# Ten channel chunks of a token-and-channel mixer as five pairs in one stage, with the first block's up-projection issued from the attention stage

## The chip, the cores and the metric

The program runs on one core of one Trainium2 chip. The metric is device time in microseconds (us). Three runs of the kernel before took 1213.01, 1213.05 and 1217.84 us; the median is 1213.05 us. All arithmetic is in 32-bit floating point. A matmul operand is split into a high and a low part, and a product of two operands is three matmuls (high by high, high by low, low by high).

## What is computed

Three blocks follow one another on 8 sequences of 576 tokens with 512 channels.

```python
# 1. memory attention: 8 sequences, 8 heads, 576 x 64, 32 memory slots
a = softmax(phi); k_m = a.T @ k; v_m = a.T @ v
x = softmax(q @ k_m.T * scale) @ v_m
# 2. mixer: tokens 576 -> 256 -> 576, channels 512 -> 1536 -> 512
u = x + (relu(x.T @ w_tok1) @ w_tok2).T
x = u + relu(u @ w_ch1) @ w_ch2
# 3. four attention heads, causal, gated: the two best of four for each token
out = sum over the chosen heads of gate * (softmax(causal(q k.T)) @ v @ wo)
```

The change concerns the channel part, `relu(u @ w_ch1) @ w_ch2`. Its 1536 hidden channels are 12 chunks of 128. An up-projection multiplies u with one chunk of `w_ch1`; a down-projection multiplies the result with the same chunk of `w_ch2` and adds it to a sum over chunks.

## The kernel before, in words

**Stage 1, attention and tokens.** The work is 16 units, one for each sequence and each half of its heads. A unit has a front (`front`, L340: phi's maximum, the exponential, k_m and v_m, q transposed), rows (`rows`, L476: scores, softmax, transposes back) and a mix (`mix`, L568: both token matmuls, then u). A unit uses every engine several times in turn: PE, DVE, ACT and POOL. The loads of phi, k, v and q go through SP (`loads`, L313); u is kept in an SBUF tile `u1` for each sequence and stored to `u_d` (`u_s`, L633).

Chunks 0 and 1 of the channel part are done here too (N1 = 2, L245). `block(j)` (L659) does one half sequence, 288 tokens: it splits u (`u_hi`, `u_lo`, L663 to L670), does two up-projections (`up`, L672; `up_hi`, `up_lo`) and four partial sums of the down-projection (`down`, L691), adds them to u (`down_c`, L696) and stores u plus the partial sum to `p_d` (`store`, L700). One block is 48 matmuls of 288 columns. There are 16 blocks. Those of the last sequence (`rest`, L734) are not planned in stage 1; they are issued at the start of stage 2 (L1068).

The weights arrive as 64-bit numbers. `convert` (L746) turns a piece into a high and a low part: one DMA into a staging tile `cst` (three of them), two ACT instructions, four DVE instructions, and a last subtraction on POOL or DVE. In stage 1 that happens to the token weights (5 pieces) and to chunks 0 to 6 of the channel weights (7 chunks, 14 pieces, `chan`, L814).

The order of stage 1 is written out ahead of time by a planner (`Plan`, L63). Each task carries an engine, an assumed duration, what it reads and writes, and a place in a ring of buffers (L304). The planner issues, on each engine, the ready task with the lowest rank: the latest start that its successors allow, or `due` where one is given. The order it finds is then kept on each engine.

**Stage 2, channels** (L898 to L1162). Nine blocks of 512 tokens are multiplied with chunks 2 to 9, as four pairs. `mm1` (L916) is the up-projection of one chunk, 12 matmuls of 512 columns; `mm2` (L1019) is the down-projection of one chunk, 12 matmuls of 512 columns into four PSUM banks. In blocks 2 to 7 (`WIDE`), `mm1w` (L980) does the two up-projections of a pair with seven products instead of eight quarter-products: 42 matmuls of 256 columns. For that, sums of weights are formed during block 1 (`sums_w`, L935) and sums of u before each wide block (`split_q`, `split_t`). A down-projection is issued one step after its up-projection. At the end of a block `load_p` (L1029) has brought u plus the partial sum from `p_d`, DVE adds the four banks, and the result goes to `x_d` (L1026, L1027). `midload` (L1062) converts the weights of chunks 7 to 9 during block 0 (`f64_split`, L223). Instructions outside the planned stage are put in order by the framework's own scheduler, which may move them ahead of their place in the text when their data and memory are free.

**Stage 3, the last two chunks and the heads** (from L1166). Chunks 10 and 11, then the third block. The change does not touch it.

Of the kernel before, what the change touches and what calls it, by code (L numbers as in the profile page):

```python
# [9 lines left out]
F32 = mybir.dt.float32  # L10
# [52 lines left out]
class Plan:  # L63
# [5 lines left out]
    def add(self, eng, ns, fn, reads=(), writes=(), take=None, n=1, kind="", due=None):  # L69
        t = dict(i=len(self.tasks), eng=eng, ns=ns, fn=fn, take=take, n=n, kind=kind, due=due, pre=set(), gives=[], holders=0)  # L70
# [19 lines left out]
    def order(self):  # L90
# [26 lines left out]
        for t in ts:  # L117
            if not left[t["i"]]:
                open_[t["eng"]].append(t["i"])
        wire, now = 0, 0  # L120
# [47 lines left out]
def fused_kernel(ctx: ExitStack, tc, q, k, v, phi, w_tok1, w_tok2, w_ch1, w_ch2,  # L168
# [19 lines left out]
    p_d = tc.dram_tile([DM, NT], F32, name="p_d")  # L188
# [56 lines left out]
    N1, NP, N3 = 2, 5, 2  # L245
    KM = KF - N3
    wch_ctx, b1_ctx, stg_ctx = ExitStack(), ExitStack(), ExitStack()
    wbm = wch_ctx.enter_context(tc.tile_pool(name="wbm", bufs=1, reuse_waits="tile"))
    wb = b1_ctx.enter_context(tc.tile_pool(name="wb", bufs=1, reuse_waits="tile", side="right"))
    wk1 = None  # L250
    ppb1 = b1_ctx.enter_context(tc.tile_pool(name="ppb1", bufs=1, space=PSUM, reuse_waits="tile", side="right"))
# [18 lines left out]
    u1, uh1, ul1, h1 = {}, {}, {}, {}  # L270

    def half(j):
        return slice(SH * (j % 2), SH * (j % 2) + SH)

    with ExitStack() as sa:
        wk1 = b1_ctx.enter_context(tc.tile_pool(name="wk1", bufs=1, reuse_waits="tile", side="right"))
        wa = sa.enter_context(tc.tile_pool(name="wa", bufs=1, reuse_waits="tile"))
        stg = stg_ctx.enter_context(tc.tile_pool(name="stg", bufs=2, reuse_waits="tile", side="right"))
        ld = sa.enter_context(tc.tile_pool(name="ld", bufs=1, reuse_waits="tile"))
        wk_ = sa.enter_context(tc.tile_pool(name="wk_", bufs=1, reuse_waits="tile"))  # L280
        pp = sa.enter_context(tc.tile_pool(name="pp", bufs=1, space=PSUM, reuse_waits="tile"))
# [17 lines left out]
        DVE.memset(kv_[ST:128, :, :, 4, :], 0.0)  # L299

        units = [(b, g) for b in range(B) for g in range(2)]
        NU, NR, NJ = len(units), 2, 2 * B
        NB = S // 32
        plan = Plan(pools=dict(t=2, g=4, b=2, cst=3, cy=2, cm=2),  # L304
# [8 lines left out]
        def loads(n):  # L313
            b, g = units[n]
            hs = slice(4 * g, 4 * g + 4)

            def l_phi():
                t, src = phb[n % NB2], phi[b, hs]
# [1332 lines left out]
```

## Time and profile before

| | before |
|---|---|
| median of three runs | 1213.05 us |
| the profiled execution: its own time | 1214.76 us |
| the profiled execution: its span | 1213.0 us |
| PE busy, share of the span | 1165.3 us, 96% |
| DVE busy | 816.3 us, 67% |
| ACT busy | 610.8 us, 50% |
| POOL busy | 449.5 us, 37% |
| mean share of the 16 DMA engines in use | 39.2% |

The profile is one execution. PE is the matmul engine, DVE the vector engine, ACT the scalar engine, POOL the general engine, SP the one that issues the DMAs here. Busy time is the union of an engine's instructions in a stretch. A granted clock of 1.00 means that PE ran at the upper of its two levels (2.4 GHz) in the whole stretch; 0.74 means that it ran at the lower one (1.2 GHz) in about half of it. The mean duration of a PE matmul in a table is longer than the distance from one to the next, since matmuls overlap; in the chain of waits the distance is seen. "PE o" are down-projections of stage 2, "PE h" its up-projections, "PE b" the matmuls of `block`.

### The profile page before, as it was taken

How to read it: one execution, taken by the hardware profiler on the slowest of the kernel's cores; microseconds unless marked ns; L12 is line 12 of the kernel's file. 1: busy time of each engine (PE TensorE's matmuls, PEld its weight loads, DVE VectorE, ACT ScalarE, POOL GpSimd, SP SyncE). 2: the span in 40 equal slices, each digit the busy share in tenths (PEclk: the TensorE clock that was granted, in tenths of full speed). 3: DMA queues.
4: the chain of work that ended last, by engine and by line, in shares of the span. 5: the costliest groups of instructions: out<-in, count | busy, mean ns of one | idle time of the engine just before them, and what ended most of it. 6: DMA issues, size and time to landing. Idle time of an engine off the chain costs nothing.

```text
span 1213.0 us, 23508 instructions
## 1 busy us (share of the span) xinstructions
PE 1165.3 (96%) x8586; PEld 1064.7 (88%) x8586; DVE 816.3 (67%) x1992; ACT 610.8 (50%) x1591; POOL 449.5 (37%) x603
## 2 busy tenths in 40 slices
PE   4899998999999999999999999999999999999998
PEld 3678887999888888889999889999999999999986
DVE  6999998665483756567566514777676767676664
ACT  3565565454442323223322213677676767677775
POOL 2774453442002012112111344545454627383331
PEclk9799999999999999999999999999999999999999
DMA  8896767532370221232123343322333333322522
GB/s 239 251 276 209 215 212 221 171 118 92 97 251 20 105 70 35 71 104 97 43 71 105 96 113 114 88 84 79 84 88 83 102 97 99 94 80 54 166 86 105
DMA packets 133780, 145.07 MB, mean 120 GB/s; under 512 B 35616, under 2 KB 101408, under 8 KB 133664
## 3 DMA queue, kind: packets, MB, share of 16 engines
q1 hardware_dynamic: 133664, 143.57, 39.2%
q8 instruction: 68, 1.11, 0.4%
q14 instruction: 48, 0.39, 0.1%
HBM read 91.10 MB, written 40.89 MB: 109 GB/s over the span
## 4 chain that ended last, share of the span: by engine, by line
PE 79%; DVE 11%; DMA 3%; issue 2%; ACT 2%; POOL 1%; SPq 0%; DVEq 0%; ACTq 0%; POOLq 0%
PE g L207 21%; PE o L207 16%; PE h L207 16%; PE y L1423 4%; PE b L207 3%; PE s L1314 3%; PE b L679 3%; PE t L1378 3%; PE s L1336 1%; DVE ul L670 1%; DVE cy L772 1%; PE g L623 1%; PE g L383 1%; PE g L624 1%; PE g L626 1%
## 5 line engine op out<-in xcount | busy, mean ns | idle before, releaser
L1359 POOL TENSOR_TENSOR a<-a,cf 128x128 f32<-128x128 f32 (+3 forms) x128 | 88.3, 723 | 68.9 <-DVE cf L1351 64.9
L207 PE MATMUL o<-hl,w2h 128*128 128x512 f32 x288 | 112.7, 391 | 0.3 <-DVE hl L931 0.3
L207 PE MATMUL o<-hh,w2l 128*128 128x512 f32 x288 | 112.3, 390 | 0.0
L207 PE MATMUL o<-hh,w2h 128*128 128x512 f32 x288 | 108.7, 392 | 0.2 <-DVE pb L1026 0.2
L930 ACT ACTIVATE hh<-m 128x256 fp32r<-128x256 f32 x96 | 38.9, 416 | 111.8 <-DVE m L1001 72.2
L1303 DVE CUSTOM_DVE_ANT_0 ssb<-s,cmask 128x128 f32<-128x128 f32 (+2 forms) x144 | 68.5, 483 | 27.3 <-PE s L1314 20.5
L1316 ACT ACTIVATE a<-ssb,nb 128x128 f32<-128x128 f32 (+3 forms) x128 | 71.3, 558 | 18.4 <-DVE nb L1303 15.1
L207 PE MATMUL h<-uh,w1h 128*128 128x512 f32 (+2 forms) x200 | 66.5, 334 | 4.7 <-ACT uh L211 4.7
L931 DVE SCALAR_TENSOR_TENSOR hl<-m,hh 128x256 fp32r<-128x256 f32 x96 | 58.2, 615 | 17.6 <-ACT hh L930 15.4
L978 POOL TENSOR_TENSOR tl<-ub,th 128x512 fp32r<-128x512 f32 x12 | 18.1, 1526 | 136.3 <-ACT th L977 136.3
L207 PE MATMUL h<-uh,w1l 128*128 128x512 f32 (+2 forms) x200 | 66.7, 334 | 0.0
L1215 POOL TENSOR_TENSOR xl<-p,xh 128x288 fp32r<-128x288 f32 x60 | 47.4, 811 | 51.8 <-ACT xh L1214 51.6
L207 PE MATMUL h<-ul,w1h 128*128 128x512 f32 (+2 forms) x200 | 66.1, 335 | 0.0
L207 PE MATMUL g<-xh,qkh 128*128 128x288 f32 x232 | 65.3, 301 | 0.0
L207 PEld LDWEIGHTS o<-hh,w2l 128*128 128x128 f32 x288 | 54.1, 188 | 11.3
L207 PE MATMUL g<-xh,qkl 128*128 128x288 f32 x232 | 63.9, 296 | 0.0
L207 PEld LDWEIGHTS o<-hh,w2h 128*128 128x128 f32 x288 | 54.0, 188 | 10.7 <-DVE pb L1026 1.0
L963 POOL TENSOR_TENSOR ub<-ub 128x512 f32<-128x512 f32 x6 | 9.8, 1628 | 144.4 <-DVE ul L214 144.4
L207 PEld LDWEIGHTS o<-hl,w2h 128*128 128x128 f32 x288 | 54.1, 188 | 10.0 <-DVE hl L931 0.6
L214 DVE TENSOR_TENSOR Bl<-t,Bh 128x512 fp32r<-128x512 f32 (+1 forms) x80 | 50.5, 633 | 14.3 <-ACT Bh L211 12.6
L923 DVE SCALAR_TENSOR_TENSOR hl<-h,hh 128x512 fp32r<-128x512 f32 x24 | 16.5, 689 | 59.9 <-ACT hh L922 59.8
L1430 POOL TENSOR_TENSOR yl<-yt,yh 128x256 fp32r<-128x256 f32 x30 | 22.2, 739 | 85.0 <-ACT yh L1429 74.9
(340 smaller groups left out, 4123.8 us busy)
## 6 DMA issues: line engine op xcount, KB each, us to landing
cst<-in_moe_w_ch_dram SPq DMA_DIRECT2D x24, 512.0 KB, 4.8
u_d<-u SPq DMA_DIRECT2D x32, 288.0 KB, 3.6
p_d<-u SPq DMA_DIRECT2D x16, 576.0 KB, 4.2
ub<-u_d SPq DMA_DIRECT2D x9, 1024.0 KB, 5.7
pb<-p_d SPq DMA_DIRECT2D x36, 256.0 KB, 4.1
x_d<-pb SPq DMA_DIRECT2D x36, 256.0 KB, 2.1
u<-u_d SPq DMA_DIRECT2D x16, 576.0 KB, 4.2
p<-x_d SPq DMA_DIRECT2D x15, 576.0 KB, 4.1
```

Of the source, the lines that this page charges most:

```text
L207: PE.matmul(ps, lhsT=a, rhs=b, start=start and i == 0, stop=stop and i == len(seq) - 1)
L214: DVE.tensor_sub(lo, src, f(hi))
L679: PE.matmul(h1[j, fc, "p"][:], lhsT=w[:, kd, :], rhs=x[:, kd, :], start=(part == 0 and i == 0), stop=(part == 1 and i == KD - 1))
L930: ACT.activation(hh, c, AF.Relu)
L931: DVE.scalar_tensor_tensor(hl, c, 0.0, f(hh), op0=OP.max, op1=OP.subtract)
L1215: POOL.tensor_sub(xl[b][:, c, ss], x_, f(xh[b][:, c, ss]))
L1303: DVE.tensor_tensor_reduce(out=out, in0=p, in1=mask, scale=-scale, scalar=least, op0=OP.add, op1=OP.min, accum_out=acc)
L1314: PE.matmul(p[:, 0:W], lhsT=q_[n][:, 128 * c:128 * c + 128], rhs=kk[n][:, 0:W], start=(i == 0), stop=(i == 1))
L1316: ACT.activation(a[:, aoff[c]:aoff[c] + W], s_[:, 0:W], AF.Exp, scale=-1.0, bias=nb[:, 0:1], accum_out=sm[:, c:c + 1])
L1359: POOL.tensor_mul(x_, x_, cf[:, c:c + 1].to_broadcast([128, W]))
L1378: PE.transpose(p[:, 128 * kc:128 * kc + 128], a[:, o + 128 * kc:o + 128 * kc + 128], ident[:])
L1423: PE.matmul(p[:, lo:w], lhsT=v_[:, kc, 0, :], rhs=x, start=(i == 0), stop=(i == len(ops) - 1))
```

## The change

- N1 = 2 is gone. Stage 1 has no channel chunks: `block`, `rest`, the store to `p_d` and the tensor itself are taken out. Chunks 0 to 9 are done in stage 2 as five pairs, for all nine blocks. `load_p` reads `u_d`. Stage 3 keeps chunks 10 and 11.
- Stage 1 converts chunks 0 to 4 (five chunks, 10 pieces, all with the last subtraction on DVE), spread by a due time of 70 us plus 12 us for each piece, before which the planner doesn't issue the load. `midload` converts chunks 5 to 9 in block 0.
- `ahead` is new. After the last unit's scores and all conversions it loads u of stage 2's block 0, splits it on ACT and DVE, and issues the up-projections of chunks 0 to 3 (48 matmuls of 512 columns) as planned tasks. In stage 2, `mm1` skips these.
- More buffers in stage 1: two tiles instead of one for k and v, for the exponentials of phi, for the scores and for the attention rows; five staging tiles instead of three. The token weights' loads get ranks of their own, ahead of unit 1's k, v and q.
- Fewer buffers in stage 2: three `pb` tiles instead of four, one `m5` instead of two; uh and ul get one tile in each of two pools, used in turn.
- u is stored from small tiles (`wu`, four of 128 x 576) instead of a tile for the whole sequence.

```diff
-        rank = [end - tail[t["i"]] if t["due"] is None else t["due"] for t in ts]
+        rank = [end - tail[t["i"]] if t["rank"] is None else t["rank"] for t in ts]
-        ready_at = [0] * len(ts)
+        ready_at = [t["due"] or 0 if t["eng"] == "SP" else 0 for t in ts]
...
-    p_d = tc.dram_tile([DM, NT], F32, name="p_d")
...
-    N1, NP, N3 = 2, 5, 2
+    NP, NA, N3 = 5, 4, 2
...
-        kv_ = ld.tile([128, 2, 4, 5, D], F32, name="kv")
+        kvb = [ld.tile([128, 2, 4, 5, D], F32, name=f"kv{i}") for i in range(NB2)]
...
-        plan = Plan(pools=dict(t=2, g=4, b=2, cst=3, cy=2, cm=2),
+        plan = Plan(pools=dict(t=2, g=4, h=2, cst=5, cy=2, cm=2),
...
-                e = st["e"] = wk_.tile([128, 4, 5, M], F32, name="ea", bufs=1)
+                e = st["e"] = wk_.tile([128, 4, 5, M], F32, name="ea", bufs=2)
...
-                    st["x"] = wk_.tile([128, NB, M], F32, name="ssb", bufs=1)
+                    st["x"] = wk_.tile([128, NB, M], F32, name="ssb", bufs=2)
...
-                st["a"] = wk_.tile([128, S], F32, name="at", bufs=1)
+                st["a"] = wk_.tile([128, S], F32, name="at", bufs=2)
...
+        def ahead():
+            def opened():
+                stg_ctx.close()
+                ld_ctx.close()
+                st["b0"] = b0_ctx.enter_context(tc.tile_pool(name="b0", bufs=1, reuse_waits="tile", side="right"))
+                load_u(0, st["b0"])
...
+            def up(fc):
+                st[fc] = ppw.tile([128, 512], F32, name="h", bufs=2)
+                mm3(st[fc][:], [((w1h[fc][:, kd, :], w1l[fc][:, kd, :]), (uh[0][:, kd, :], ul[0][:, kd, :]))
+                                for kd in range(KD)])
...
+            add("SP", (600, 4300), opened, reads=[("ud", 0), ("ud", 1)], writes=["ub"], after=[U[NU - 1]["score"], *convs])
+            for kd in range(KD):
+                add("ACT", 600, lambda kd=kd: s_hi(kd), reads=["ub"], writes=[("bh", kd)])
+                add("DVE", 700, lambda kd=kd: s_lo(kd), reads=["ub", ("bh", kd)], writes=[("bl", kd)])
+            for fc in range(NA):
+                a = add("PE", 12 * 227, lambda fc=fc: up(fc), reads=[(x, kd) for x in ("bh", "bl") for kd in range(KD)] + [("w1", fc)],
+                        writes=[("up", fc)], take="h")
...
+        L0[0] = [0, 1, 2, 3]
+        L0[1] = [4, 5000, 5001, 5002]
...
-            if n == 1:
-                for i in range(2):
-                    for fc in range(N1):
-                        chan(i, fc, None)
-            if n % 2:
-                block(n - 1)
-                block(n)
-        c = 0
-        for fc in range(N1, N1 + NP):
-            for i in range(2):
-                chan(i, fc, 150000 + 15000 * c)
-                c += 1
+        for c in range(2 * NP):
+            chan(c % 2, c // 2, 70000 + 12000 * c)
+        ahead()
...
-            f0, f1 = N1 + 2 * q, N1 + 2 * q + 1
+            f0, f1 = 2 * q, 2 * q + 1
...
-            pb[n, c] = wk_.tile([128, 512], F32, name="pb", bufs=4)
-            SP.dma_start(pb[n, c][:], p_d[128 * c:128 * c + 128, 512 * n:512 * n + 512])
+            pb[n, c] = wk_.tile([128, 512], F32, name="pb", bufs=3)
+            SP.dma_start(pb[n, c][:], u_d[128 * c:128 * c + 128, 512 * n:512 * n + 512])
...
-            for fc in range(N1 + NP, KM):
+            for fc in range(NP, KM):
                 yield from ch_weights(wb2, stg, fc, DM, 2)
...
-        load_u(0)
-        for i, piece in enumerate(rest):
-            with tc.high_priority():
-                piece()
-            if i < 20:
-                next(wcl, None)
-        for kd in range(KD):
-            split_u(0, kd)
-        load_u(1)
+        load_u(1, wk_)
+        for _ in range(8):
+            next(wcl, None)
...
-        NQP = (KM - N1) // 2
+        NQP = KM // 2
```

## Rows read from the trace of the kernel before

**Rows 1.** The page, busy time, share of the span and instructions of each engine.

```profile
PE 1165.3 (96%) x8586; PEld 1064.7 (88%) x8586; DVE 816.3 (67%) x1992; ACT 610.8 (50%) x1591; POOL 449.5 (37%) x603
```

**Rows 2.** Busy time by stage; columns as the first line names them.

```profile
core 0: us, PE busy (x) PEld busy (x) DVE busy (x) ACT busy (x) POOL busy (x), PEclk, DMA share, GB/s
0.00:60.00 60.00, 39.58 (x443) 30.25 (x444) 47.53 (x89) 27.87 (x59) 31.39 (x44) 0.86 0.88 244
60.00:200.00 140.00, 133.81 (x1356) 118.20 (x1355) 136.19 (x254) 83.99 (x198) 73.66 (x84) 1.00 0.72 220
200.00:329.50 129.50, 124.53 (x1110) 114.32 (x1109) 75.11 (x164) 59.72 (x146) 35.49 (x43) 0.97 0.42 134
329.50:393.80 64.30, 59.59 (x292) 51.21 (x291) 36.66 (x68) 22.16 (x43) 6.06 (x4) 0.97 0.43 142
393.80:728.60 334.80, 334.36 (x1946) 295.26 (x1946) 195.92 (x383) 85.47 (x188) 72.69 (x77) 1.00 0.26 82
```

**Rows 3.** The chain of waits: start us, us, what.

```profile
1.31 4.12 DMA phb<-in_phi_dram
...
111.26 8.12 DMA qn<-in_q_dram
...
309.56 1.59 PE b L207 x12
...
329.73 5.69 DMA ub<-u_d
...
335.44 0.64 ACT uh L211
...
391.06 2.72 PE o L207 x12
...
456.49 4.11 PE o L207 x18
...
466.97 4.10 PE o L207 x18
...
728.56 1.59 PE h L207 x12
```

**Rows 4.** Groups of matmuls of `block` in the first 330 us.

```profile
L207 PE MATMUL b<-hh,w2h 128*128 128x288 f32 x112 | 33.5, 314 | 1.1 <-DVE hl L688 1.0
L679 PE MATMUL b<-uh,w1h 128*128 128x288 f32 x120 | 33.3, 303 | 0.0
L679 PE MATMUL b<-uh,w1l 128*128 128x288 f32 x119 | 32.3, 296 | 0.0
L207 PE MATMUL b<-hh,w2l 128*128 128x288 f32 x112 | 31.4, 295 | 0.0
...
L207 PE MATMUL b<-hl,w2h 128*128 128x288 f32 x112 | 24.1, 295 | 0.2 <-DVE hl L688 0.2
...
L679 PE MATMUL b<-ul,w1h 128*128 128x288 f32 x112 | 18.0, 300 | 0.0
```

**Rows 5.** Groups of DVE instructions in the first 330 us.

```profile
L670 DVE TENSOR_TENSOR ul<-u,uh 128x288 fp32r<-128x288 f32 x60 | 38.5, 666 | 7.3 <-PE b L679 4.0 <-ACT uh L667 3.1
L698 DVE TENSOR_TENSOR u<-u,b 128x288 f32<-128x288 f32 x56 | 24.4, 445 | 10.1 <-PE b L207 9.8
...
L772 DVE SCALAR_TENSOR_TENSOR cy<-cst,cm 128x512 int32<-128x512 int32 (+2 forms) x19 | 19.8, 1050 | 0.1
L769 DVE SCALAR_TENSOR_TENSOR cm<-cm,cy 128x512 int32<-128x512 int32 (+2 forms) x19 | 14.9, 797 | 0.0
...
L761 DVE TENSOR_SCALAR cm<-cm 128x512 f32<-128x512 f32 (+2 forms) x19 | 12.6, 673 | 0.1
...
L688 DVE SCALAR_TENSOR_TENSOR hl<-b,hh 128x288 fp32r<-128x288 f32 x28 | 11.8, 441 | 13.5 <-ACT hh L684 13.4
...
L765 DVE TENSOR_SCALAR cy<-cst 128x512 int32<-128x512 uint32 (+2 forms) x19 | 10.8, 584 | 0.0
```

**Rows 6.** DMA totals and issues of the first 329.5 us: count, KB each, us to landing.

```profile
DMA packets 68996, 62.82 MB, mean 191 GB/s; under 512 B 16480, under 2 KB 63072, under 8 KB 68960
...
cst<-in_moe_w_ch_dram SPq DMA_DIRECT2D x18, 512.0 KB, 5.4
...
qn<-in_q_dram SPq DMA_DIRECT2D x16, 512.0 KB, 6.5
p_d<-u SPq DMA_DIRECT2D x14, 576.0 KB, 4.2
```

**Rows 7.** Stretches of 20 us in stage 1, columns as in rows 2.

```profile
20.00:40.00 20.00, 14.61 (x173) 11.35 (x174) 19.72 (x36) 8.22 (x18) 12.92 (x15) 0.74 0.83 235
40.00:60.00 20.00, 16.43 (x159) 13.08 (x158) 18.69 (x34) 13.92 (x31) 15.46 (x20) 0.83 0.86 238
60.00:80.00 20.00, 18.74 (x221) 16.16 (x220) 19.34 (x37) 14.42 (x36) 14.43 (x15) 1.00 0.98 284
80.00:100.00 20.00, 17.98 (x189) 15.40 (x188) 19.68 (x35) 11.55 (x28) 13.17 (x16) 1.00 0.67 211
...
200.00:220.00 20.00, 15.61 (x148) 13.58 (x147) 15.68 (x33) 10.57 (x25) 7.74 (x10) 0.83 0.92 269
```

**Rows 8.** SP's issues in order of time: start us, us, line, what.

```profile
25.42 0.35 SPq L810 DMA_DIRECT2D cst<-in_moe_w_tok_dram  x1
...
61.53 1.68 SPq L635 DMA_DIRECT2D u_d<-u  x2
...
330.20 0.52 SPq L635 DMA_DIRECT2D u_d<-u  x1
...
336.30 0.38 SPq L262 DMA_DIRECT2D cst<-in_moe_w_ch_dram  x1
...
359.72 0.34 SPq L264 DMA_DIRECT2D cst<-in_moe_w_ch_dram  x1
```

**Rows 9.** What SP's queue waited for in the first 330 us: total us, times, longest.

```profile
SPq L325 <- PE g L383: 25.1, 9, 8.6
...
SPq L810 <- DVE cy L772: 4.4, 2, 4.1
```

**Rows 10.** The page's DMA issues of stage 2, KB each, median us to landing.

```profile
pb<-p_d SPq DMA_DIRECT2D x36, 256.0 KB, 4.1
x_d<-pb SPq DMA_DIRECT2D x36, 256.0 KB, 2.1
```

More of the change, by code (lines that the diff above doesn't have):

```diff
@@ L79, in add @@
             self.wrote[k] = t["i"]
+        t["pre"] |= {x["i"] for x in after}
         t["pre"].discard(t["i"])
@@ L653, in mix @@
                     es.append(add("ACT", 410, lambda c=c, hf=hf: u_c(c, hf), reads=[(n, "u", c, hf)],
[L654 removed]
+                                  writes=[("u", (2 * n + c) % 4, hf)]))
                 free(a, *es)
             for c in range(2):
[L657 to L680 removed]
@@ L691, in down @@
-            def down(c):
-                p = h1[j, "d", c] = ppb1.tile([128, SH], F32, name="b", bufs=2)
-                mm3(p[:], [((w2h[fc][:, c, :], w2l[fc][:, c, :]), (h1[j, fc, 0][:], h1[j, fc, 1][:]))
-                           for fc in range(N1)], late="r")
-            def down_c(c):
-                u_ = u1[b][:, c, ss]
-                DVE.tensor_add(u_, u_, h1[j, "d", c][:])
-            def store():
-                SP.dma_start(p_d[:, SH * j:SH * j + SH].rearrange("(c p) s -> p c s", p=128), u1[b][:, :, ss])
@@ L716, in piece_d @@
-            def piece_d(c):
-                a = add("PE", 6 * MM, lambda: down(c), reads=[("fh", 0), ("fl", 0), ("fh", 1), ("fl", 1), ("w2", 0), ("w2", 1)],
-                        writes=[(j, "d", c), ("dn", c)], take="b")
-                e_ = add("DVE", 455, lambda: down_c(c), reads=[(j, "d", c), ("u1", b % 2, c, hf)],
-                         writes=[("u1", b % 2, c, hf)])
-                free(a, e_)
-                if c == KD - 1:
-                    add("SP", (600, 1800), store, reads=[("u1", b % 2, kd, hf) for kd in range(KD)])
@@ L744, in fused_kernel, with convert @@
         weights = [0]
-        def convert(load, ns, P, n, out, key, early):
+        STG = 5
+        def convert(load, ns, P, n, out, key, early, rank=None):
             st = {}
@@ L828, in out @@
                 return [x[:].rearrange("p c f -> p (c f)") for x in (h_[fc], l_[fc])]
-            convert(ld, (600, 1650), 128, DM, out, (nm, fc), due)
-        PJ, TOK_DUE = False, None
-        U, rest = {}, []
+            convert(ld, (600, 1650), 128, DM, out, (nm, fc), due, due)
+        PJ, TOK_DUE, TOK_RANK = False, None, 3000
+        U, convs = {}, []
+        L0 = {n: [None] * 4 for n in range(NU)}
+        L0[0] = [0, 1, 2, 3]
+        L0[1] = [4, 5000, 5001, 5002]
         for n in range(NU):
@@ L1107, in fused_kernel @@
                         if n == 0:
-                            next(wcl, None)
-                        if n == 1:
+                            for _ in range(8):
+                                next(wcl, None)
+                        if n == 1 and fc > 0:
+                            if sw is None:
+                                stg_ctx.close()
+                                b0_ctx.close()
+                                sw = sw_ctx.enter_context(tc.tile_pool(name="sw", bufs=1, side="right", reuse_waits="tile"))
+                                stmp = tmp_ctx.enter_context(tc.tile_pool(name="stmp", bufs=1, side="right", reuse_waits="tile"))
                             with tc.issue_after(latest(DVE)):
```

239 lines of the change are left out of this document (102 added, 137 removed).

## The prediction

> **What bounds the kernel now.** The page comes first: PE is busy for 96% of the span, DVE for 67% [rows 1]. So time is saved by fewer or cheaper matmuls, or by fewer holes between them. The busy times by stage say where the holes are [rows 2]. From 393.8 us to the end of stage 2 PE lacks 0.4 us in 334.8. All the slack lies in stage 1 and at its seam. In 0 to 329.5 us PE is idle for 20.4 + 6.2 + 5.0 = 31.6 us. It also ran at the lower clock for a while: a mean of 0.86 over 60 us loses 0.14 x 60 = 8.4 us, and 0.97 over 129.5 us loses 3.9 us. In the 64.3 us after it PE is idle for another 4.7 us, and the chain of waits shows why: stage 2's first block waits 5.69 us for u, and for ACT's split behind it [rows 3].
>
> Stage 1 has two halves. Up to 200 us DVE is the fuller engine: 47.53 of 60 and 136.19 of 140 us, while PE has 133.81 of 140. After it DVE falls to 75.11 of 129.5 and PE is the bound [rows 2]. So `block` does two things there: it fills PE, and it loads the DVE that the attention units wait for.
>
> **What is removed.** One block is 48 matmuls of 288 columns. In the chain twelve of them take 1.59 us [rows 3], 0.133 us each, so 6.4 us a block; 687 stand in stage 1 [rows 4], 91.4 us, and the two blocks left over make 12.8 us more in stage 2. On DVE the groups of `block` sum to 38.5 + 24.4 + 11.8 = 74.7 us [rows 5]. Four of the 14 chunk pieces also leave stage 1: 1.05 + 0.80 + 0.67 + 0.58 = 3.1 us of DVE each, 12.4 us. The stores to `p_d` go, 14 of 576 KB in stage 1 [rows 6].
>
> **What is added.** Each block of stage 2 gets a fifth pair. A plain pair is two up- and two down-projections of 2.72 us, 10.88 us; a wide pair is the distance from 456.49 to 466.97 us, 10.48 us [rows 3]. For blocks 1 to 8 that is 6 x 10.48 + 2 x 10.88 = 84.6 us.
>
> **Stage 1 after.** I take PE as its bound. Its busy time to 329.5 us is 39.58 + 133.81 + 124.53 = 297.9 us [rows 2]; less 91.4 for the blocks and 12.3 for the lower clock, 194.2 us belong to the 16 units, 12.1 us each. The four early up-projections add 4 x 2.72 = 10.9 us. The start costs what it cost: 20.4 us idle and 8.4 us of clock in the first 60 us. Together 233.9 us.
>
> Two things are left out of this sum, taken as equal. For a better start: the loads of the last two token weights were issued only from 25.42 us on [rows 8], behind a staging tile [rows 9], and five tiles free them. Against it: without the blocks PE has nothing to put into a unit's waits. It was idle for 11.2 us between 60 and 329.5 us even with them. The ends are far apart. The low end is every hole closed but the first load, which lands at 1.31 + 4.12 = 5.4 us [rows 3]: 205.1 + 5.4 = 210.5 us. The high end, without a better start and with the later losses twice over (11.2 idle, 3.9 clock), is 233.9 + 30.2 = 264 us. I take 233.9, the value nearest to the rows of the first 60 us.
>
> The other engines don't set a later end. DVE: 258.8 us in stage 1, less 74.7 and 12.4, plus eight instructions of the early block at about 0.69 us, 177 us. ACT and POOL were at 171.6 and 140.5 us and only lose work. DMA: 62.82 MB [rows 6] less 14 x 0.59 for `p_d` and 8 x 0.52 for the chunk pieces (18 become 10), plus 1.05 MB for u, 51.4 MB. At 284 GB/s, the rate of the stretch with a share of 0.98 [rows 7], that is 181 us. Each of these is 50 us or more below 234, which is the margin for waiting on one another. The double tiles for k and v take away what SP's queue waited for most among the loads, 25.1 us for the single one [rows 9]; the loads queued behind it on SP then move up as well.
>
> **The seam and block 0.** The load of u and ACT's split now run while the last unit's rows are on DVE, ACT and POOL. If that cover is gone it costs 335.44 + 0.64 - 329.73 = 6.4 us [rows 3]. Before, block 0 ends at 393.78 us with the last "PE o" [rows 3], one up-projection of block 1 being done already. After, 10 down-projections, 6 up-projections and that one of block 1 remain: 17 x 2.72 = 46.2 us. `midload` now has ten pieces instead of six there. Before, six were issued from 336.30 to 359.72 us [rows 8], 4.7 us each. Two can be read and begun ahead; the ninth piece (chunk 9's up-projection) is then ready after some 7 x 4.7 + 3 = 36 us, and PE needs it after 13 x 2.72 = 35.4 us. I take 1 us; the ends are 0 and 7 us (all ten behind the last unit).
>
> **Three `pb` tiles.** Four pieces of u are needed at a block's end, so the fourth load now waits for the first store to `x_d`. Store, load and two additions take 2.1 + 4.1 + 2 x 0.7 us [rows 10], with about 0.4 us for each issue some 8.4 us after the first bank's last matmul. PE returns to the fourth bank after three more banks, the next up-projections and three banks again, 2.0 + 5.0 + 2.0 = 9 us. What is queued behind this wait on SP is the next load of u, which has a block's time. I take 2 us over all blocks, between 0 and 8. The single `m5` and the alternate uh, ul tiles: nothing, since each is rewritten only a pair (10 us) or two blocks later.
>
> **The sum.** Stage 2's last pair ends at 728.56 us before. After: 233.9 + 46.2 + 1 + (728.6 - 393.8 = 334.8) + 84.6 + 2 = 702.5 us. Stage 3 is unchanged. That is 26.1 us less. Against the profiled execution, 1214.76 us, it makes 1188.7 us; that execution is 1.7 us above the median of the runs, so at the median 1213.05 - 26.1 = 1187.0 us.
>
> Half of the saving is matmul time: 91.4 + 12.8 against 84.6 and block 0's 10.9, some 9 us. The 5 us of the seam and DVE's relief in stage 1 make the rest, and that is where it can fail. The point from which it decides is T1, the end of stage 1's matmuls: 233.9 forecast, 260.0 break-even.
>
> **Rivals.**
> - The units close up: T1 between 210.5 and 217, 1164 to 1170 us. For it: DVE, full up to 200 us, loses a third of its work. Against: units whose work goes round four engines rarely leave PE without holes.
> - The units keep their distance (slower). From the first store of u at 61.53 us to the last at 330.20 us a unit takes 17.9 us [rows 8]; the forecast needs (233.9 - 61.5) / 15 = 11.5, break-even is 13.2. The place is q's tile, still single: its load took 8.12 us on the chain at 111 us [rows 3], 6.5 in the median [rows 6], and waits for the transposes of the unit before; DMA was at 0.98 already from 60 to 80 us [rows 7]. At 14.7 us, halfway, T1 is 282 and the time 1235 us. Against: the 17.9 us hold 6.4 us of block on PE and 4.7 us on DVE.
> - The clock. In the stretches of 20 us where PE was busy for 14.61, 16.43 and 15.61 us the granted clock was 0.74, 0.83, 0.83; where it was busy for 17.98 it stayed at 1.00 [rows 7]. 205 us of work in 234 us is 17.5 of 20, between these. A fall to the lower level at the price of the last of them is 0.17 x 20 = 3.4 us, so eight more falls undo the gain; six make 1207 us. For it: fewer matmuls between the waits. Against: the fullest waits were at the start. The Trainium skill ("TensorE: Matmul & The Clock Gate", section "Why this matters for your kernels") advises against idle gaps between bursts of matmuls, since the engine returns to half rate after them. By that rule, with a fall in each of the 16 units, T1 would be 288 and the time 1241 us; the trace agrees as far as its three low stretches go, but 80 to 100 us has holes too and keeps its clock.
> - The early part comes late: the up-projections stand behind the last unit's matmuls, the load isn't covered (6.4 us), and the conversions and `pb` cost their upper ends (6 more each): about 1205 us. That is also the case in which the change doesn't do what it says, for the planner fixes the order by assumed durations.
>
> **How the numbers follow.** The forecast has 0.47, the units closing up 0.17, the late seam 0.13, the clock 0.12, the kept distance 0.11. The likeliest case alone spans 1176 to 1200 us. The range goes down to T1 = 210.5 (1163 us) and up to about no change (1214 us), which leaves out most of the kept distance and the worst of the clock. About 0.5% (6 us) can be told from no change, so T1 has to stay below 254 for faster. Faster: 0.47 + 0.17 + 0.13 and a third of the clock case, 0.81. Same: 0.06. Slower: 0.13.
>
> **What would show it.** In the profile after: stage 1's matmuls end near 234 us, with DVE near 177 us in it; the stores of u stand 11 to 12 us apart; the first "PE o" follows the last unit without a wait for u; stage 2's pairs still take 10.5 and 10.9 us; between blocks PE waits less than 1 us for an addition into `pb`. Units 13 us apart or more, PE waiting for q, or many low stretches in the granted clock would make it wrong; so would waits of stage 2 for converted weights.

## The result, and the profile after

The changed kernel is slower: 1229.3 us median of 4 runs (1224.3 to 1231.2) beside 1213.3 us, a ratio of 1.012 [1.008, 1.016]. In a second set of runs it took 1222.4 us, 1.010 [1.007, 1.013]. The forecast was 1187 us, with 1163 to 1214 as its range.

The busy time by stage of the profiled execution comes first (span 1227.0 us, own time 1228.8). Its bounds are the ones of [rows 2], moved to where the stages now end: the last matmul of stage 1 at 255.5 us (329.5 before), block 0's end at 305.3 (393.8), stage 2's last pair at 737.2 (728.6).

```profile
core 0: us, PE busy (x) PEld busy (x) DVE busy (x) ACT busy (x) POOL busy (x), PEclk, DMA share, GB/s
0.00:60.00 60.00, 33.84 (x438) 26.04 (x439) 42.01 (x78) 22.99 (x49) 28.53 (x41) 0.89 0.88 237
60.00:207.00 147.00, 140.45 (x1564) 118.04 (x1562) 127.63 (x241) 95.70 (x225) 94.73 (x115) 0.99 0.77 227
207.00:255.50 48.50, 44.67 (x297) 38.43 (x282) 19.86 (x36) 19.33 (x42) 8.01 (x10) 0.96 0.34 117
255.50:305.30 49.80, 47.22 (x204) 37.97 (x203) 35.05 (x57) 17.51 (x31) 6.20 (x4) 1.00 0.40 131
305.30:737.24 431.94, 420.68 (x2428) 369.83 (x2427) 233.99 (x470) 104.31 (x230) 73.19 (x76) 0.99 0.23 70
737.24:1227.00 489.76, 475.70 (x3450) 456.81 (x3449) 327.00 (x1037) 333.24 (x958) 230.02 (x354) 0.99 0.32 93
sum 1227.00, PE 1162.56 PEld 1047.12 DVE 785.54 ACT 593.08 POOL 440.68; mean PE 193.76 PEld 174.52 DVE 130.92 ACT 98.85 POOL 73.45
```

Idle time of PE is the first number less the second. Blocks 1 to 8 were the tightest stretch before, with 0.4 us idle in 334.8 [rows 2]. Now they have 11.3 in 431.9. Stage 1 has 26.2 + 6.6 + 3.8 us against 20.4 + 6.2 + 5.0. In all PE is busy for 1162.6 us against 1165.3 [rows 1]: 228 matmuls fewer, but 2.7 us instead of the 9 us forecast.

The trade is then: stage 1 and block 0 are 393.8 - 305.3 = 88.5 us shorter, blocks 1 to 8 are 431.9 - 334.8 = 97.1 us longer, stage 3 is 489.8 - 484.4 = 5.4 us longer. Together 14 us lost.

T1, the end of stage 1, at 255.5 us, stands before the forecast's break-even of 260.0. Taken alone it would have left a gain of 4.5 us; blocks 1 to 8 and stage 3 turned it into a loss.

Where the new idle time in stage 2 comes from is told by what PE waited for between 305 and 737 us (engine, line, releaser: total us, times, longest):

```profile
PE o L209 <- DVE pb L980: 7.8, 5, 2.6
PE h L209 <- DVE m L961: 2.8, 1, 2.8
```

The same addition in the kernel before (393 to 729 us), and below it the start of stage 3 there (720 to 760 us):

```profile
PE o L207 <- DVE pb L1026: 0.2, 1, 0.2
...
PE g L207 <- DVE p L1213: 0.6, 1, 0.6
```

`DVE pb L980` is the addition of the down-projection's bank into the piece of u at a block's end. Its wait was 0.2 us in the whole of stage 2 before. The second row after, 2.8 us, is one wait at 365 us, in the first wide block; the kernel before has none there. One end of a block, on DVE (start, us, line, operation, idle time before it):

```profile
471.51 2.62 DVE L885 SCALAR_TENSOR_TENSOR hl<-m,hh 128x256 fp32r<-128x256 f32 x2
474.05 0.68 DVE L980 TENSOR_TENSOR pb<-o,pb 128x512 f32<-128x512 f32 x1
474.65 0.92 DVE L885 SCALAR_TENSOR_TENSOR hl<-m,hh 128x256 fp32r<-128x256 f32 x1
475.50 1.28 DVE L980 TENSOR_TENSOR pb<-o,pb 128x512 f32<-128x512 f32 x2
...
480.36 0.69 DVE L980 TENSOR_TENSOR pb<-o,pb 128x512 f32<-128x512 f32 x1 [2.07 <-DMA pb<-u_d]
480.97 0.42 DVE L885 SCALAR_TENSOR_TENSOR hl<-m,hh 128x256 fp32r<-128x256 f32 x1
```

and the chain of waits over the same microseconds (start, us, what):

```profile
474.13 0.04 DVE pb L980
...
477.22 3.05 DMA pb<-u_d
...
480.36 0.70 DVE pb L980
...
481.10 3.01 PE o L209 x12
```

Three additions run, the fourth waits. With three `pb` tiles for four pieces, the fourth load is issued at 477.22 us, after the first addition (474.05 to 474.73) and the store of its tile. The addition follows when it has landed, and PE, which had come back to the fourth bank at some 479.8 us, stands until 481.1. VectorE (DVE) keeps its order here: the `hl` of the next pair, whose `hh` was done at 478.80 us, stands behind the waiting addition and starts at 480.97.

The same chain ends stage 2, and there stage 3's first split is behind it:

```profile
741.37 0.70 DVE pb L980
...
742.09 2.06 DMA x_d<-pb
...
744.16 2.80 DMA pb<-u_d
...
747.08 0.06 DVE pb L980
...
747.69 1.56 DVE ul L216 x4
749.24 0.37 DVE p L1167
```

PE waits 4.1 us for that `p` (L1167). Before, the wait for the same line was 0.6 us.

### The profile page after: what moved, and what is told of

It reads as the page before. It is cut to its first block, busy times and chain, and to the rows that moved or that the text cites. A ratio compares the mean times of both kernels' runs of the same rounds, so it can differ in the third digit from the quotient of the medians.

```text
span 1227.0 us, 22877 instructions
## 1 busy us (share of the span) xinstructions
PE 1162.6 (95%) x8358; PEld 1047.1 (85%) x8358; DVE 785.5 (64%) x1917; ACT 593.1 (48%) x1533; POOL 440.7 (36%) x599
## 4 chain that ended last, share of the span: by engine, by line
PE 71%; DVE 12%; DMA 8%; ACT 3%; issue 3%; POOL 2%; SPq 0%; DVEq 0%; ACTq 0%; POOLq 0%
PE g L209 22%; PE o L209 15%; PE h L209 14%; PE y L1377 4%; PE s L1268 3%; PE t L1332 3%; DMA ub<-u_d 3%; DVE ul L216 1%; DMA cst<-in_moe_w_ch_dram 1%; PE s L1290 1%; PE g L387 1%; DMA pb<-u_d 1%; DVE hl L885 1%; PE g L621 1%; POOL tl L932 1%
## 5 line engine op out<-in xcount | busy, mean ns | idle before, releaser
L209 PE MATMUL o<-hh,w2h 128*128 128x512 f32 x360 | 138.2, 397 | 8.6 <-DVE pb L980 7.8
L209 PE MATMUL o<-hl,w2h 128*128 128x512 f32 x360 | 141.4, 393 | 2.0 <-DVE hl L877 1.8
L209 PE MATMUL o<-hh,w2l 128*128 128x512 f32 x360 | 140.5, 390 | 0.0
L209 PEld LDWEIGHTS o<-hh,w2h 128*128 128x128 f32 x360 | 68.0, 190 | 24.1 <-DVE pb L980 9.3
L209 PE MATMUL h<-uh,w1h 128*128 128x512 f32 (+2 forms) x248 | 83.4, 337 | 2.8 <-DVE m L961 2.8
L209 PE MATMUL h<-uh,w1l 128*128 128x512 f32 (+2 forms) x248 | 83.2, 336 | 0.0
L209 PE MATMUL h<-ul,w1h 128*128 128x512 f32 (+2 forms) x248 | 82.4, 336 | 0.0
L209 PEld LDWEIGHTS o<-hl,w2h 128*128 128x128 f32 x360 | 67.7, 188 | 14.8 <-DVE hl L877 2.2
L209 PEld LDWEIGHTS o<-hh,w2l 128*128 128x128 f32 x360 | 67.6, 188 | 14.4
L1169 POOL TENSOR_TENSOR xl<-p,xh 128x288 fp32r<-128x288 f32 x60 | 47.5, 811 | 65.5 <-ACT xh L1168 64.1
L209 PEld LDWEIGHTS h<-uh,w1h 128*128 128x128 f32 x248 | 47.0, 190 | 10.5 <-DVE m L961 3.0
L948 ACT ACTIVATE m<-h 128x256 f32<-128x256 f32 x30 | 11.5, 384 | 88.0 <-PE h L209 88.0
```

The costliest lines, as they stand in the source:

```text
L209: PE.matmul(ps, lhsT=a, rhs=b, start=start and i == 0, stop=stop and i == len(seq) - 1)
L1169: POOL.tensor_sub(xl[b][:, c, ss], x_, f(xh[b][:, c, ss]))
```

## The experiments

Theories before the first runs: **A**, the three `pb` tiles hold every block's end; **B**, the additions into `pb` come late because DVE has more in front of them; **C**, the start of stage 1 is held by the order of its loads. Later expectations use the same letters for theories of their own. This table gathers all runs. T1 is the start of the last copy of u out of stage 1, T2 the first matmul into g of stage 3's own (from hh, w2h); the rest are stretches between them and PE's idle time, in us, of one profiled execution each.

| kernel | median | ratio to before | T1 | T1 to T2 | T2 to end | PE idle 0–60 / 60–T1 / T1–T2 |
|---|---|---|---|---|---|---|
| before | 1213.3 | | 329.3 | 405.0 | 478.7 | 20.4 / 11.2 / 5.2 |
| changed | 1229.3 | 1.012 | 255.5 | 487.5 | 484.1 | 26.2 / 10.4 / 13.8 |
| changed, again | 1222.4 | 1.010 | 256.8 | 480.1 | 482.7 | 26.8 / 10.6 / 8.7 |
| fourth `pb` tile | 1213.8 | 1.002 | 256.1 | 476.7 | 478.6 | 26.4 / 9.5 / 6.7 |
| single products | 1227.6 | 1.012 | 256.5 | 485.5 | 484.5 | 26.5 / 10.1 / 12.3 |
| before, 3 `pb` tiles | 1212.4 | 1.000 | 321.9 | 405.7 | 486.8 | 20.4 / 7.5 / 6.2 |
| token loads first | 1220.5 | 1.007 | 252.8 | 484.4 | 482.6 | 22.1 / 10.0 / 10.9 |
| both of these edits | 1209.2 | 0.998 | 249.3 | 480.1 | 477.2 | 22.7 / 10.2 / 7.9 |
| single unit tiles | 1220.2 | 1.007 | 255.1 | 479.4 | 482.3 | 33.3 / 6.5 / 7.6 |
| no early ups | 1221.4 | 1.008 | 251.9 | 482.1 | 481.5 | 25.7 / 7.4 / 9.8 |
| both and fence | 1202.7 | 0.993 | 247.6 | 475.1 | 477.7 | 21.9 / 8.2 / 4.6 |
| fence alone | 1218.3 | 1.006 | 250.7 | 480.5 | 483.8 | 27.2 / 8.1 / 8.8 |
| repaired, no early ups | 1207.0 | 0.996 | 250.5 | 479.3 | 476.9 | 20.7 / 8.1 / 7.7 |
| repaired, single unit tiles | 1210.4 | 0.998 | 248.1 | 483.3 | 477.9 | 27.9 / 10.5 / 6.2 |

**The changed kernel again.**

> The changed kernel itself once more, as the measure for the others of this call. Theory A: the chip plays no part and the ratio to the kernel before is 1.010 to 1.014, so some 1226 us against 1212. Theory B: part of what the experiments gave back is the chip's, and the ratio is under 1.008.

1222.4 us, ratio 1.010 [1.007, 1.013]: the low edge of theory A, with B not excluded. It tells what a difference has to be to count. The same program's two profiles are 7.4 us apart. T1 came 1.3 us later in the second and stage 3 was 1.4 shorter; the 7.4 lie between T1 and T2, where the waits for the fourth piece were 7.8 us in the one and 4.4 in the other. So gains are read against 1222 to 1229, and from the stretch in which the edit works. The two executions have the same instructions in the same order on every engine, and so have the next two kernels in the table up to 300 us; their T1 lie between 255.5 and 256.8.

**A fourth tile for the blocks' pieces.** It takes memory that is free until stage 3 needs it, and the product tiles become single to make room.

```
-  m1, u2_, u3, u4, c = [... bufs=1 if x == "m5" else 2 ...]
+  m1, u2_, u3, u4, c = [... bufs=1 ...]
...
+  if n and c == KD - 1:
+      pb[n, c] = (sw if n <= WIDE[-1] else w3).tile([128, 512], F32, name="pbx", bufs=1)
```

> The changed kernel with a tile of its own for the fourth piece of u in blocks 1 to 8, so that its load no longer waits for the first store to x_d (room is made by one tile instead of two for m1 to m4). Theory A, the missing fourth pb tile makes PE's holes in blocks 1 to 8 (11.3 us idle from 305.3 to 737.2 us, 0.4 us before the change) and most of the 5.4 us that stage 3 lost: 12 to 16 us faster than the changed kernel, about 1215 us, PE idle under 2 us in blocks 1 to 8. Rival B, the additions into pb come late because DVE has more in front of them (the split of u and the hidden rows of five pairs): within 3 us of the changed kernel.

1213.8 us, ratio 1.0016 [1.0006, 1.0026]. The stores and loads on SP at a block's end (start, us, line, operation) stand so now:

```profile
472.29 2.35 SPq L981 DMA_DIRECT2D x_d<-pb  x3
...
475.24 0.40 SPq L981 DMA_DIRECT2D x_d<-pbx  x1
```

The fourth store is issued 3.0 us after the first, where it was at 481.08, 6.3 us after. And by stage:

```profile
0.00:60.00 60.00, 33.60 (x434) 25.89 (x435) 41.42 (x78) 22.79 (x48) 28.36 (x41) 0.72 0.91 235
60.00:256.08 196.08, 186.62 (x1849) 158.07 (x1849) 147.32 (x277) 115.56 (x267) 102.38 (x124) 0.97 0.66 200
256.08:732.73 476.65, 469.92 (x2664) 412.56 (x2663) 271.00 (x529) 124.29 (x267) 80.10 (x82) 1.00 0.24 77
732.73:1211.32 478.59, 467.65 (x3415) 450.02 (x3413) 325.08 (x1035) 331.17 (x952) 229.22 (x352) 1.00 0.33 95
```

T1 hasn't moved, the stretch to T2 is 3.4 to 10.8 us shorter, and stage 3 takes 478.6 us, what it took before (478.7). So 8 to 16 us of span are this tile's, 4 to 5.5 of them at the seam. Theory A holds, and theory B's number (within 3 us) doesn't. PE no longer waits for `pb` from 305 to 737 us. One thing of A was missed: it had under 2 us of idle time left in blocks 1 to 8, and the wait for `m` (L961) at 365 us grew from 2.8 to 4.2 us. No run took that wait away.

**The product tiles alone.**

```
-  m1, u2_, u3, u4, c = [... bufs=1 if x == "m5" else 2 ...]
+  m1, u2_, u3, u4, c = [... bufs=1 ...]
```

> The changed kernel with one tile instead of two for m1 to m4 and nothing else: what the room for the fourth pb tile costs by itself. Both theories: within 3 us of the changed kernel, since each of these tiles is rewritten a pair (10 us) later.

1227.6 us, ratio 1.012 [1.011, 1.014]: no difference from the changed kernel, as both theories had it. So the gain of the fourth tile isn't that of the single products. This kernel is also its nearest comparison, from the same set of runs and with the tile as the only edit between them: 1227.6 and 1213.8 us, 13.8 us.

**The kernel before with three tiles.**

```
-  pb[n, c] = wk_.tile([128, 512], F32, name="pb", bufs=4)
+  pb[n, c] = wk_.tile([128, 512], F32, name="pb", bufs=3)
```

> The kernel before with three pb tiles instead of four, nothing else. Theory A: 10 to 16 us slower than before, 1223 to 1229 us, since the wait stands at the end of each block and doesn't depend on the number of pairs. Rival B (DVE's load from five pairs): within 3 us of before.

1212.4 us, ratio 1.000 [0.999, 1.001]: theory A's number missed, and B's (within 3 us) came. The stages tell why A isn't refuted (against [rows 2]):

```profile
200.00:329.50 129.50, 126.49 (x1127) 115.82 (x1119) 73.44 (x162) 60.77 (x151) 34.44 (x43) 1.00 0.41 132
329.50:393.80 64.30, 64.30 (x309) 54.48 (x309) 48.11 (x88) 24.48 (x43) 9.18 (x6) 1.00 0.53 175
393.80:728.60 334.80, 331.04 (x1941) 292.00 (x1940) 188.37 (x371) 84.01 (x188) 70.47 (x74) 1.00 0.24 76
```

The expected waits are there: idle time in 393.8 to 728.6 us is 3.8 instead of 0.4, PE waits for `pb` 3.5 us in 4, and stage 3 takes 486.8 instead of 478.7 us, 5.9 us of it a wait for `p` at the seam that was 0.6. But the program isn't the old one otherwise. The 4.7 us in which PE waited for u at the seam are gone, the granted clock from 200 us on is 1.00 instead of 0.97, and T1 comes 7.4 us sooner. The framework's scheduler had laid other instructions differently around one tile less: on DVE the order is another from 204 us on. The two cancel within 1 us; how much of the 7.4 us is the order, and how much the spread between executions, isn't shown. One edit in such a program isn't one difference, and only the stages could tell the parts.

**The token loads first.** The token weights come in five pieces, two of them the second token weights (L772). The edit issues these two in the first group, not behind two more units' k and v.

```
-  convert(ld, (600, 1750), 128, S, ..., ("t2", c), TOK_DUE, TOK_RANK + 10 + c)
+  convert(ld, (600, 1750), 128, S, ..., ("t2", c), TOK_DUE, 5 + c)
```

> The changed kernel with the loads and conversions of w_tok2 ranked ahead of unit 1's k, v, q. Theory C, stage 1 starts worse than before (26.2 us of PE idle in the first 60 us, 20.4 before; first store of u at 69 instead of 62 us) because the second tiles for k and v let loads of units 1 to 3 go ahead of w_tok2, whose conversion then stands at the head of DVE's and ACT's queues: first store of u at 60 to 63 us, 5 to 8 us faster than the changed kernel. Rival D, the start is bound by the bytes that units 0 to 2 need, in whatever order: within 3 us.

1220.5 us, ratio 1.007 [1.005, 1.008]. In the changed kernel the load is SP's at 24.43 us, and a unit's early transpose stands behind the late conversion (the loads on SP; the group of matmuls in 0 to 60 us, its idle time last):

```profile
7.60 1.41 SPq L761 DMA_DIRECT2D cst<-in_moe_w_tok_dram  x2
9.38 1.14 SPq L765 DMA_DIRECT2D cst<-in_moe_w_tok_dram  x2
...
24.43 1.36 SPq L772 DMA_DIRECT2D cst<-in_moe_w_tok_dram  x2
...
L364 PE MATMUL t<-ident,pmc 128*128 128x128 f32 x6 | 2.4, 399 | 8.9 <-DVE pmc L360 8.9
```

With the edit:

```profile
7.92 1.23 SPq L772 DMA_DIRECT2D cst<-in_moe_w_tok_dram  x2
9.86 0.38 SPq L761 DMA_DIRECT2D cst<-in_moe_w_tok_dram  x1
...
25.97 0.68 SPq L761 DMA_DIRECT2D cst<-in_moe_w_tok_dram  x1
26.70 1.46 SPq L765 DMA_DIRECT2D cst<-in_moe_w_tok_dram  x2
...
L364 PE MATMUL t<-ident,pmc 128*128 128x128 f32 x6 | 2.5, 412 | 0.6 <-DVE pmc L360 0.6
```

The 8.9 us are down to 0.6, but PE's wait for v grew from 6.0 to 8.3 us, and the idle time of the first 60 us fell by 4.1. T1 moved by 2.7 to 4.0 us, theory C's place and a part of its size: the first store of u came at 65.5 us where C had 60 to 63, and against the second measurement the time is only 1.9 us shorter, rival D's number.

The two groups of rows show something else. The edit didn't bring all the token loads forward; it changed which of them are late. In both kernels three of the five pieces are issued by 10 us and two wait until after 24 (the two loads of L765 are one piece). The text of the changed kernel says why. By rank its late pieces (3010 and 3011, L774 and L794) stand ahead of unit 1's k, v and q (5000 to 5002, L798). But `room` (L107), which asks whether a ring has a tile free, cuts its list of earlier users at `len(ring) + n - size`. For the fourth piece in a ring of five that is -1, and in Python the list then holds the first two pieces instead of none. So the fourth piece waits until those are converted, as if its tile weren't there (in the changed kernel VectorE is done with the second at 22.34 us, and the load goes at 24.43). With three tiles, as before, the same slip has no effect. No run repaired this test, so what it costs isn't shown.

**Both edits.**

> The changed kernel with two edits together: the own tile for a block's fourth piece of u (14 us in the run that had it alone, 1213.8 us against about 1227.6) and the loads of the second token weights taken first (1220.5 us alone, some 8 us). Theory A: the two losses lie in different stretches (the boundaries of the blocks after 305 us, and the first 60 us) and add up: 1204 to 1208 us, 0.5% under the kernel before, with PE's idle time after 305 us as with the own tile alone and the first store of u near 65 us. Theory B: the framework's scheduler moves other instructions in answer to either edit, as it did when a tile was taken from the kernel before, and what one edit gives the other loses: 1211 to 1216 us.

1209.2 us, 0.998 [0.996, 0.999]. The gains lie in the stretches where each was alone (T1 249.3, stage 3 477.2 us), and come to 5 us more than the tile's alone, where 8 were expected. But the sooner T1 isn't the pair's doing: up to 300 us every engine has the same instructions in the same order as with the loads alone, where T1 was 252.8. The 3.5 us between the two are spread between executions, and the granted clock is part of it (0.92 and 1.00 from 207 to 250 us). The idle time between T1 and T2 is 1.2 us longer than with the tile alone, from waits in block 0. So theory A, with a little of B.

**The unit's second tiles taken away.**

```
-  kvb = [ld.tile([128, 2, 4, 5, D], F32, name=f"kv{i}") for i in range(NB2)]
+  kvb = [ld.tile([128, 2, 4, 5, D], F32, name=f"kv{i}") for i in range(1)]
...
-  e = st["e"] = wk_.tile([128, 4, 5, M], F32, name="ea", bufs=2)
+  e = st["e"] = wk_.tile([128, 4, 5, M], F32, name="ea", bufs=1)
```

(likewise the score rows and the attention rows)

> The changed kernel with stage 1's second tiles of k and v, e, the score rows and the attention rows taken away again, all else as it is (five load tiles, pairs, early up-projections). Theory A: without the chunks' matmuls between them the units are held by these tiles, so that single ones put idle time between the units: the stores of u lie more than 12.6 us apart (12.2 with two tiles), the last matmul of stage 1 comes after 260 us instead of 255.5, and the time is over 1235 us. Theory B: TensorE is busy for 140.5 of 147 us there, and the tiles free only what the loss of 6.6 us could give back at most: within 3 us of 1228.

1220.2 us, 1.007 [1.006, 1.009], no different from the changed kernel's second measurement. T1 is 255.1 us. PE is idle for 7 us more in the first 60 and for 4 less after. So the second tiles brought the start nothing that stage 1's end shows, and theory B comes nearer.

**No early up-projections by the plan.**

```
-  NP, NA, N3 = 5, 4, 2
+  NP, NA, N3 = 5, 0, 2
```

> The changed kernel with none of block 0's up-projections put between the last units (the conversions of its u stay there): the 11 us of matmuls come behind stage 1 instead. Theory A: they fill idle time of the last four units, 3.8 us of which is left in 207 to 255.5 us with them: without them the stretch to the last unit shortens by less than the 11 us, and the time is 4 to 9 us longer (1232 to 1237). Theory B: they only take the place of the units' own work, one for one: stage 1 ends 11 us sooner, block 0 is 11 us longer, and the time is within 2 us of 1228. Theory C: they hold the last units up by more than their own length: the time falls by over 2 us.

1221.4 us, 1.008 [1.006, 1.010], again like the second measurement. It isn't the removal it was meant to be: the trace shows 60 up-projections of block 0 between 200 and 256 us, as many as in the changed kernel. The framework's scheduler interleaves them by itself. By the numbers put down this would be theory C, a fall of over 2 us from 1228; against the second measurement it is no difference. The plan's own order is worth nothing here that the runs could tell.

**VectorE's first conversions for stage 2 kept behind stage 1.**

```
-  for _ in range(8):
-      next(wcl, None)
+  with tc.issue_after(latest(DVE)):
+      for _ in range(8):
+          next(wcl, None)
```

What it aims at is in the tail of stage 1, 207 to 250 us of the changed kernel (a window, then waits of PE, DVE and ACT):

```profile
207.00:250.00 43.00, 39.17 (x262) 33.63 (x247) 19.86 (x36) 18.10 (x39) 8.01 (x10) 0.96 0.38 129
...
PE g L630 <- DVE hl L612: 2.9, 1, 2.9
...
DVE cm L235 <- ACT cm L234: 4.7, 2, 3.8
...
ACT cm L234 <- DMA cst<-in_moe_w_ch_dram: 7.2, 3, 4.3
```

and VectorE in order of time:

```profile
222.49 0.68 DVE L612 SCALAR_TENSOR_TENSOR hl<-g,hh 128x512 fp32r<-128x512 f32 x1
...
229.22 0.43 DVE L235 TENSOR_SCALAR cm<-cm 128x512 f32<-128x512 f32 x1 [3.79 <-ACT cm L234]
229.70 0.69 DVE L537 TENSOR_TENSOR alo<-t,ahi 128x512 fp32r<-128x512 f32 x1
```

ACT waits for a load of stage 2's weights and VectorE for ACT, 3.8 us, with `alo` of the last unit queued behind. The `hl` at 222.49 us, for which PE waits 2.9 us, stands behind seven instructions of such conversions, from 214.96 us on, and among them four splits (`ul`) of the early part's u.

> As the kernel with both edits, and VectorE's part of the first conversions for stage 2 kept behind stage 1's last instruction on that engine; in the changed kernel the scheduler moved them into the last units, where VectorE waited on their loads and TensorE on the instructions behind. Theory A: this is where TensorE's last gaps of stage 1 come from (3.8 us idle in 207 to 255.5 us): 2 to 4 us faster than with both edits. Theory B: the conversions had idle time of VectorE there and none now: they collide with block 0's, and the time is the same or up to 5 us longer.

With both edits and the fence: 1202.7 us, 0.993 [0.992, 0.995], 5 to 7 us under both edits alone, more than either theory had. Only 1.7 us of it lie before T1 (249.3 to 247.6); the other 4.9 lie between T1 and T2.

> The changed kernel with the fence alone (VectorE's part of the first conversions for stage 2 behind stage 1's last instruction on that engine). Behind the two other edits it gave 6.6 us: the end of stage 1 came 1.7 us sooner (249.31 to 247.62 us), and 4.9 us of it lay in block 0 and 1, where the waits of the second matmuls on the first hidden rows (1.1 and 0.5 us) and on an issue (2.0 us) were gone. Theory A: the conversions in stage 1's tail are a loss of their own: 5 to 8 us faster than the changed kernel. Theory B: where the order in which the scheduler interleaves is what decides, the gain belongs to that one combination: within 3 us of the changed kernel.

Alone: 1218.3 us, 1.006 [1.004, 1.008], 4 us under the second measurement. Its window:

```profile
207.00:250.00 43.00, 42.27 (x285) 36.49 (x278) 18.70 (x34) 18.03 (x39) 7.61 (x9) 1.00 0.32 113
```

Idle time of 0.7 us instead of 3.8, 23 more matmuls in the same stretch, the granted clock 1.00 instead of 0.96, and T1 at 250.7 us, 5 to 6 sooner. ACT's wait for the load fell from 7.2 to 0.6 us. So the conversions in the tail are a loss of their own (theory A), by the window and T1. The time alone wouldn't show it: 4 us lie between the two theories (5 to 8, within 3), and the two ratios' intervals overlap.

By stage, the kernel with all three edits, which beats both kernels:

```profile
0.00:60.00 60.00, 38.15 (x460) 28.92 (x460) 44.37 (x86) 26.76 (x56) 29.59 (x45) 0.94 0.96 252
60.00:247.62 187.62, 179.46 (x1824) 151.14 (x1823) 143.38 (x266) 111.37 (x257) 100.16 (x120) 1.00 0.67 201
247.62:722.74 475.12, 470.57 (x2665) 413.40 (x2664) 271.55 (x531) 125.50 (x269) 79.84 (x82) 0.99 0.24 79
722.74:1200.43 477.69, 467.60 (x3415) 450.14 (x3413) 326.08 (x1035) 330.45 (x952) 228.92 (x352) 1.00 0.33 95
```

**What the change's own parts are worth once this is repaired.**

> The kernel with all three edits (1202.7 us), and no early up-projections by the plan. Alone this gave the changed kernel about 6 us: stage 1 ended 3.6 us sooner, and the framework's scheduler put 60 of the same matmuls (5 chunks of 12) between the last units all the same. Theory A: the plan's early ups only cost, whatever else is repaired: 1197 to 1200 us. Theory B: their gain lay in the waits at the block boundaries (idle time from stage 1's end to that of stage 2 fell from 13.8 to 9.8 us), which the fourth tile has already removed, and in the place of the conversions: within 2 us of 1202.7 or slower.

> The kernel with all three edits (1202.7 us) and stage 1's tiles single. Alone this left the end of stage 1 where it was (255.1 against 255.5 us) and took 6.3 us of idle time out of stage 2, 3.5 us of it from the waits for the fourth piece. Theory A: with the fourth tile in place nothing of that is left to gain: within 3 us of 1202.7, which would show that the second tiles are worth nothing in stage 1. Theory B: with the start repaired the units are near enough to each other for the single tiles to hold them: stage 1 ends later than 250 us (247.6 with two) and the time is over 1206 us.

Without the plan's early ups 1207.0 us, 0.996 [0.994, 0.998]; with single unit tiles 1210.4 us, 0.998 [0.997, 0.999]; with neither edit 0.993 [0.992, 0.995]. The second tiles are thus worth some 5 to 8 us there, theory B's time. Its place was wrong: T1 is 248.1 us, but 23 matmuls fewer lie before it and so more behind it (2688 between T1 and T2 instead of 2665), and the first 60 us have 27.9 us of idle time instead of 21.9. The early ups look worth 3 to 4 us (theory A falls), though the two intervals touch. In the changed kernel itself neither showed any worth.

## Why the prediction was wrong

In the profile the forecast missed by 40.1 us (1186.9 for the span, 1227.0 measured). By its own terms:

| term | forecast | measured | difference |
|---|---|---|---|
| T1, end of stage 1's matmuls | 233.9 | 255.5 | +21.6 |
| block 0 with conversions | 47.2 | 49.8 | +2.6 |
| blocks 1 to 8 with `pb` | 421.4 | 431.9 | +10.5 |
| stage 3 | 484.4 | 489.8 | +5.4 |

**The step that failed most is T1**, and in it the sentence that took the later holes as equal to a better start. The holes after 60 us were 10.4 us, near the 11.2 of before and in no way cancelled. The start didn't get better but worse: 26.2 us idle where 20.4 were carried over. Five staging tiles did not bring the last token weights forward. They were issued at 24.43 us (25.42 before [rows 8]). What held them was no longer a tile but the planner's own test for a free one, read from its text and from two orders of the loads, not from a run without it. I had taken the number of tiles for the order. The rest of T1 is 3.8 us of more matmul time, 2.7 of them a fifth up-projection of block 0 that the scheduler put ahead of T1 (60 such matmuls, not 48), and 1.6 us of clock. The runs moved T1 by 3 to 7 us with the loads (two executions of the same stage 1) and by 5 to 6 us with the fence, to 247.6 with both. What keeps the other 13.7 us from 233.9 is 8.2 us of holes between 60 us and T1, 1.5 us at the start, and the rest more, longer or slower matmuls; no run took the holes apart, so their cause is open.

**The `pb` term was mis-sized**: 2 us, with 8 as the upper end. PE's waits for these additions were 7.8 us in one profile and 4.4 in the other, 4 to 5.5 more came at the seam, and the fourth tile gave back 8 to 16 us of span; the waits don't account for all of that. The mechanism was right, and so was PE's return to the fourth bank, 9 us after the first bank's last matmul (about 470.5 to 479.8 us). The chain was put at 8.4 us and took 10.6 (470.5 to 481.06). Store and load were no slower than assumed. The first addition was: it began at 474.05 us, 3.5 us after its bank was done, because VectorE was busy until then with the split of the next block's u (landed only at 467.57 us), the products and `hl` of the next pairs. A boundary of the kernel before shows the same: there the first addition starts at 483.75 us, over 4 us after its bank. And a second price was left out: at the end of stage 2 the same chain stands ahead of stage 3's first split (4 to 5.5 us), which I had put down as unchanged. The single `m5` was put at nothing; whether the 2.8 us at 365 us are its price isn't shown.

**What was right.** DVE in stage 1: 42.0 + 127.6 + 19.9 = 189.5 us against 177 forecast, no bound. The early part: u was loaded from 206.7 us on and its up-projections done between 228.7 and 251.5 us, so block 0 didn't wait for u. Block 0's 2.6 us of idle time are within the conversions' ends of 0 to 7, but PE waited there for hidden rows (`hl`, `hh`, at 279 and 291 us), not for a converted weight; the number came out by luck. The matmul saving: 9 us forecast; the repaired kernel has 1155.8 us of PE busy against 1165.3, 9.5 less. In the changed kernel only 2.7 of it appeared. Neither is a clean check: PE's busy time grows with the lower clock (from 207 to 250 us 246 matmuls took 40.4 us at 0.92 with the loads first, 261 took 40.2 at 1.00 with both edits), and the means were 0.988 before, 0.986 changed and 0.994 repaired. And the forecast's 9 count 15 matmuls twice: stage 1's 687 are 14 blocks of 48 and 15 of the two left over, which it prices again. Without them its own prices give 6.7 us; the sum for T1 and for the end isn't touched by this.

**The rivals.** The late seam had `pb` right (8 us, 7.8 measured), but its load of u was covered, block 0 lost 2.6 us where it had 7, and it forgot stage 3. The kept distance was right in sign: the stores of u are (255.9 - 69.2) / 15 = 12.4 us apart, between the 11.5 of the forecast and the 13.2 of break-even. Its place, the tile of q, was not: PE waits for q 0.2 us in the whole of stage 1. The clock: lost in stage 1 were 10.0 us against 8.4, not six more falls. The Trainium skill advises against idle gaps between bursts of matmuls ("TensorE: Matmul & The Clock Gate", section "Why this matters for your kernels"); I had read it as a fall in each unit. From 60 to 207 us, with 6.6 us of holes, none longer than 1.6, the granted clock was 0.99. The tail settles nothing: from 207 to 250 us the clock was 0.96 with 3.8 us of holes and 1.00 with the fence's 0.7, but 0.92 with the loads alone and 1.00 with both edits, the same instructions with 2.6 and 2.8 us of holes.

## What to carry to other kernels

A ring of buffers one short of what a group's end needs turns a store and a load into one serial chain at each end. Price it from when the consuming engine really reaches the first of them in its order, and follow it into the next stage. When filler work is taken out of a stage, keep every hole that the trace shows in the sum; don't cancel it against an improvement that no row shows. A buffer more gives nothing until the order of issue shows that it is used. And where a scheduler reorders, read an experiment by stages, since one edit moves more than it names.

## What the runs showed that I had not expected

The clock of the first 60 us costs almost nothing here. The changed kernel ran them at a mean granted clock of 0.89 with 438 matmuls done, its second profile at 0.72 with 429, the kernel without early ups at 1.00 with 428. Up to 210 us the three have the same instructions in the same order, and they issue the load of block 0's u at 206.7, 208.0 and 206.1 us. PE waits for loads and for DVE there, and slower matmuls fill time that was idle. So the 8.4 us that the forecast booked for the clock there were not a term of their own.

Instructions that a scheduler moves ahead are not free even on an engine with idle time: in the tail of stage 1 DVE was busy for 19.9 of 43 us, and with conversions waiting there for their weights T1 came 5 to 6 us later than with the fence alone, though only 1.7 us later where the two other edits were in place.
